# Attention's output leaves PSUM by one plain copy per chunk; rms_g is applied with the reciprocal root on VectorE

## The chip, the cores and the metric

The kernel runs on one core of a Trainium2 chip. The metric is the device time of one execution in microseconds (us), as the median of several runs. The engines are TensorE (PE in the profile; PEld is its weight load), VectorE (DVE), ScalarE (ACT), GpSimd (POOL) and SyncE (SP), each with a queue of its own that it works through in order.

## The reference

Linear attention with a decay per head, followed by a gated layer with RMS normalisation and a second layer:

```python
# _attn_ref, per step t; B, H, S, D = 2, 8, 768, 64
state = gamma * state + k_t v_t^T
y[t] = q_t state / sqrt(D)
# x: y as (B * S, H * D) = (1536, 512)
rms = np.sqrt(np.mean(x * x, axis=-1, keepdims=True) + 1e-06)
xn = x / rms * rms_g
g = xn @ w_gate
silu = g * (1.0 / (1.0 + np.exp(-g)))
x = (silu * (xn @ w_val)) @ w_out          # w_gate, w_val: 512 x 1536
h = x @ w_in                               # w_in: 512 x 2048
out = np.maximum(0.01 * h, h) @ w_out2
```

All of it is in float32; `rms_g` has one value for each of the 512 features.

## The kernel before

The 1536 tokens are cut into 12 chunks of 128. Each chunk's attention output `y` is one PSUM bank of 128 partitions by 4 x 128: features lie on the partitions in four groups of 128 (two heads each), tokens along the free dimension. Three blocks of four chunks make the buffers `xg` (float32, 128 x 4 x 512), and each block is then split into two parts for the matrix products, a rounded high part `xh` and the rest `xl`.

Up to some 67 us the attention of late chunks, the normalisation of earlier ones, the conversion of the first weights and the first products of the layer run side by side. The order of all of this is written out by hand in a table of short tokens (`ORDER`, from L49), which is issued under a manual schedule: each engine gets its instructions in the order of the tokens. What follows the table (from about 92 us on some engines) is planned in the program and ordered automatically. The normalisation of a pair of chunks passes these steps, with the token's name in brackets:

- squares (`sq`, L325) on ScalarE: the square of `y`, one instruction per chunk.
- gains (`xg`, L333) on ScalarE: `y` times `rms_g` into `xg`, one instruction for each of the four feature groups, since the gain is a per-partition scalar that differs between groups.
- first_sum and second_sum (`fa`, `sa`, L340 and L345) on VectorE: the squares of the four feature groups added together.
- total (`to`, L354) on TensorE: the sum over the partitions; mean (`me`, L361) on VectorE; rsqrt (`rs`, L365) on GpSimd, a power of -0.5.
- spread (`sp`, L371) on TensorE: the reciprocal root copied to all partitions, into the PSUM bank `norm`.
- scaled (`xs`, L388) on VectorE: `xg` times `norm` in place, for both chunks and all four groups in one instruction of 128 x 1024.
- high (`hi`, L395) on ScalarE and rest (`lo`, L402) on VectorE: the split into `xh` and `xl`.

The tokens of a pair carry the pair's number, so that `xs4` is scaled of chunks 8 and 9. The matrix products of the layer's first half are the matmuls of L657: eight on `xh`, then four on `xl`. L1062 multiplies the activated gate product by the value product, L258 is the decay mask on the attention scores, and L534 to L560 convert weights. The pairs stand in the table as `xs0` to `xs5`; the table's lines 54 to 58 hold five of them:

```
he7 v0:H xs0 kd10 he6 me1 sa5 g1:3 sc10 v0:L sq6 g1:4 sq7 ou9 fa6 xg6 sc11 rs1 up9 ds10 xg7 yi8 ds11 g1:H yi9 hi0 qs11
ou10 o0:P he8 lo0 to2 up10 sq8 he9 fa7 xg8 sa7 sa6 me2 g1:L to3 sq9 sp1 fa8 rs2 me3 xg9 yi10 xs1 rs3 v1:P yi11 fa9
o0:1 sa9 hi1 sp2 v1:1 sa8 he10 v1:2 xs2 he11 sq10 v1:3 xg10 layers Mg00 lo1 hi2 v1:4 Ng00 sq11 lo2 o1:P Mg10 fa11 xg11
fa10 o1:1 sa10 sa11 v1:H Ng10 o0:2 o1:2 Cg00 v1:L sp3 Cg10 o1:3 to4 xs3 Mv00 me4 o0:3 hi3 o1:4 Nv00 lo3 o1:H Mv10 o1:L
Cv00 rs4 o0:4 Uo00 sp4 Lo00 o0:H to5 Nv10 g2:P xs4 Mg01 me5 o0:L hi4 rs5 Cv10 lo4 Uo10 sp5 g3:P Ng01 Lo10 Mg11 xs5
```

`Mg00` is the high half and `Ng00` the low half of the first product of the layer.

Of the kernel before, what the change touches and what calls it, by code (L numbers as in the profile page):

```python
# [13 lines left out]
AF = mybir.ActivationFunctionType  # L14
ALU = mybir.AluOpType
AX = mybir.AxisListType

P = 128
CH = 128
# [47 lines left out]
def chain_kernel(ctx: ExitStack, tc: tile.TileContext, qk_t, kv, w1, w2, mask, qdec, kdec, sdec, rms_g, ident, out):  # L67
    nc = tc.nc
    NCHUNK = kv.shape[0]
    NPAIR = 4  # L70
# [31 lines left out]
    g_sb = const.tile([P, NPAIR, 1], F32, name="g_sb")  # L102
# [10 lines left out]
    def acc_bank(i, name):  # L113
        return ps_acc.tile([P, 512], F32, tag=f"acc{i}", name=name)
# [4 lines left out]
    def by_pair(t):  # L119
        return t.rearrange("p (a t) -> p a t", a=NPAIR)  # L120


    ch = {}
    xh, xl, xg = {}, {}, {}
# [17 lines left out]
    nrm = {"bank": acc_bank(3, "norm")}  # L142
# [65 lines left out]
    def block_of(c):  # L208
        return max(i for i in range(NB) if offs[i] <= c * CH)
# [117 lines left out]
    def gains(c):  # L327
        b = block_of(c)
        if b not in xg:
            xg[b] = xp.tile([P, NPAIR, BLOCKS[b]], F32, tag=f"acc{b}", name=f"xg{b}")  # L330
        o = c * CH - offs[b]
        for a in range(NPAIR):
            nc.scalar.activation(  # L333
                out=xg[b][:, a, o:o + CH], in_=ch[c]["y"][:, a * CH:(a + 1) * CH], func=AF.Copy, scale=g_sb[:, a, :]
            )

    def first_sum(c):
        s = ch[c]
# [40 lines left out]
    def span(cs):  # L379
        b = block_of(cs[0])  # L380
        o = cs[0] * CH - offs[b]
        return b, slice(o, o + len(cs) * CH)

    def scaled(cs):
        b, o = span(cs)
        x = xg[b][:, :, o]
        r = nrm[cs]["bank"][:, None, :len(cs) * CH].to_broadcast([P, NPAIR, len(cs) * CH])
        nc.vector.tensor_tensor(out=x, in0=x, in1=r, op=ALU.mult)  # L388

    def high(cs):  # L390
        b, o = span(cs)
# [923 lines left out]
    def layers():  # L1315
# [3 lines left out]
    by_chunk = {  # L1319
        "sc": scores, "ds": decay_scores, "yi": before, "ou": outer, "up": update, "kd": decay_k, "qs": decay_q,  # L1320
        "he": heads, "wm": lambda c: keep_warm(c, 4), "sq": squares, "xg": gains, "fa": first_sum, "sa": second_sum,
    }
    by_pair_of = {"to": total, "me": mean, "rs": rsqrt, "sp": spread, "xs": scaled, "hi": high, "lo": rest}
    alone = {
        "open": reopen, "layers": layers, "load": lambda: load("q11", "k11"),
# [136 lines left out]
```

## Time and profile before

| | us |
|---|---|
| median of 3 runs | 576.85 (576.67 to 576.88) |
| profiled execution, its own time | 577.89 |
| span of that execution | 576.1 |
| busy: TensorE | 567.6 (99%) |
| busy: VectorE | 501.7 (87%) |
| busy: ScalarE | 408.2 (71%) |
| busy: GpSimd | 42.8 (7%) |

A busy share is an average over the whole span. What a change is worth is read from the stretch in which it lies: who waits there, and for whom. In a list of instructions the second number is the duration; the distance to the next start can be shorter, since an instruction may start before the one ahead of it has ended.

### The profile page before, as it was taken

How to read it: one execution, taken by the hardware profiler on the slowest of the kernel's cores; microseconds unless marked ns; L12 is line 12 of the kernel's file. 1: busy time of each engine (PE TensorE's matmuls, PEld its weight loads, DVE VectorE, ACT ScalarE, POOL GpSimd, SP SyncE). 2: the span in 40 equal slices, each digit the busy share in tenths (PEclk: the TensorE clock that was granted, in tenths of full speed). 3: DMA queues.
4: the chain of work that ended last, by engine and by line, in shares of the span. 5: the costliest groups of instructions: out<-in, count | busy, mean ns of one | idle time of the engine just before them, and what ended most of it. 6: DMA issues, size and time to landing. Idle time of an engine off the chain costs nothing.

```text
span 576.1 us, 8549 instructions
## 1 busy us (share of the span) xinstructions
PE 567.6 (99%) x3091; PEld 466.5 (81%) x3091; DVE 501.7 (87%) x983; ACT 408.2 (71%) x747; POOL 42.8 (7%) x49
## 2 busy tenths in 40 slices
PE   8999999999999999999999999999999999999997
PEld 6888788888888888888788878788888788888886
DVE  8899989985776899985899999999999979995692
ACT  4799768987656556976647699989858885676330
POOL 3341300010000000010000200000100020002100
PEclk9999999999999999999999999999999999999999
DMA  8991422442211122226220322123512343101555
GB/s 341 406 353 38 147 73 75 146 147 73 74 53 32 63 74 66 81 84 136 73 75 0 91 56 96 54 89 129 180 41 74 113 85 96 39 0 27 120 88 133
DMA packets 35114, 59.28 MB, mean 103 GB/s; under 512 B 19264, under 2 KB 19520, under 8 KB 35072
## 3 DMA queue, kind: packets, MB, share of 16 engines
q1 hardware_dynamic: 31584, 51.39, 26.8%
q0 software_dynamic: 3200, 7.34, 6.2%
q8 instruction: 24, 0.39, 0.3%
q14 instruction: 18, 0.15, 0.1%
q10 hardware_dynamic: 288, 0.01, 0.0%
HBM read 50.34 MB, written 8.39 MB: 102 GB/s over the span
## 4 chain that ended last, share of the span: by engine, by line
PE 79%; DVE 8%; DMA 7%; ACT 4%; issue 1%; POOL 0%; DVEq 0%; ACTq 0%; POOLq 0%
PE X L913 11%; PE Z L913 8%; PE i L657 7%; PE ao L692 7%; PE iX L1116 7%; PE ap L692 6%; PE v L657 6%; PE g L657 6%; PE vX L1116 4%; PE gX L1116 4%; PE iZ L1116 3%; PE vZ L1116 2%; PE ao L775 2%; PE gZ L1116 2%; DMA raw_v<-in_w 2%; DMA qkv<-in_kv 2%
## 5 line engine op out<-in xcount | busy, mean ns | idle before, releaser
L692 PE MATMUL ap<-w_p,gp_0h 128*128 128x512 f32 (+1 forms) x128 | 38.8, 383 | 0.0
L657 PE MATMUL i<-x2h,w_i 128*128 128x512 f32 x128 | 31.9, 389 | 0.0
L657 PE MATMUL g<-xh,w_g 128*128 128x512 f32 x128 | 31.8, 390 | 0.0
L657 PE MATMUL v<-xh,w_v 128*128 128x512 f32 x128 | 31.7, 390 | 0.0
L657 PEld LDWEIGHTS g<-xh,w_g 128*128 128x128 f32 x128 | 23.9, 188 | 5.2 <-issue 0.2
L657 PEld LDWEIGHTS i<-x2h,w_i 128*128 128x128 f32 x128 | 24.0, 188 | 5.0
L657 PEld LDWEIGHTS v<-xh,w_v 128*128 128x128 f32 x128 | 23.9, 188 | 5.0
L692 PEld LDWEIGHTS ap<-w_p,gp_0h 128*128 128x128 f32 x128 | 23.8, 188 | 4.8
L692 PE MATMUL ap<-w_p,gp_0l 128*128 128x512 f32 x64 | 24.5, 382 | 0.0
L1052 ACT ACTIVATE more<-i 128x512 f32<-128x512 f32 x16 | 9.5, 596 | 20.0 <-PE i L657 20.0
L692 PE MATMUL ao<-go_0h,w_o 128*128 128x512 f32 x64 | 21.0, 389 | 0.0
L1116 PE MATMUL iX<-th,w_si 128*128 128x512 f32 x64 | 20.6, 399 | 0.2 <-ACT is L1133 0.2
L1116 PE MATMUL iZ<-x2h,w_si 128*128 128x512 f32 x64 | 20.5, 392 | 0.0
L560 DVE TENSOR_TENSOR w_o<-wa_o,w_o 128x512 fp32r<-128x512 f32 x12 | 8.2, 687 | 13.8 <-ACT w_o L556 13.8
L657 PE MATMUL g<-xl,w_g 128*128 128x512 f32 x64 | 17.2, 391 | 0.0
L657 PE MATMUL v<-xl,w_v 128*128 128x512 f32 x64 | 17.2, 391 | 0.0
L944 DVE TENSOR_TENSOR y2acc<-X,y2acc 128x512 f32<-128x512 f32 x26 | 17.1, 684 | 0.0
L657 PE MATMUL i<-x2l,w_i 128*128 128x512 f32 x64 | 17.1, 389 | 0.0
L258 DVE TENSOR_TENSOR a<-sc,mask_sb 128x1024 f32<-128x1024 f32 (+1 forms) x13 | 14.5, 1137 | 1.1 <-PE sc L246 1.0
L983 POOL DMA_DIRECT2D out<-more x8 | 7.1, 1030 | 113.6 <-ACT more L979 113.4
L1116 PEld LDWEIGHTS iX<-th,w_si 128*128 128x128 f32 x64 | 11.7, 188 | 4.2 <-ACT is L1133 1.2
L609 ACT ACTIVATE wb_i<-raw_i 128x512 int32<-128x512 uint32 x16 | 10.7, 671 | 5.8 <-DMA raw_i<-in_w 2.4
(385 smaller groups left out, 1860.2 us busy)
## 6 DMA issues: line engine op xcount, KB each, us to landing
raw_i<-in_w SPq DMA_DIRECT2D x16, 512.0 KB, 3.5
raw_g<-in_w SPq DMA_DIRECT2D x12, 512.0 KB, 3.6
raw_v<-in_w SPq DMA_DIRECT2D x12, 512.0 KB, 3.5
raw_o<-in_w SPq DMA_DIRECT2D x12, 512.0 KB, 3.5
raw_p<-in_w SPq DMA_DIRECT2D x11, 512.0 KB, 3.5
qkT<-in_qk_t SPq DMA_DIRECT2D x7, 512.0 KB, 8.4
kv<-in_kv SPq DMA_DIRECT2D x7, 512.0 KB, 9.2
out<-more POOLq DMA_DIRECT2D x12, 256.0 KB, 4.6
```

The source lines that it names most:

```text
L258: nc.vector.tensor_tensor(out=s["a"][:, j], in0=s["sc"][:, j], in1=mask_sb[:, j], op=ALU.mult)
L560: v.tensor_tensor(out=u[:, 1, :], in0=a, in1=u[:, 0, :].bitcast(F32), op=ALU.subtract)
L609: nc.scalar.activation(out=m, in_=low.bitcast(U32), func=AF.Copy, scale=2.0 ** -29)
L657: nc.tensor.matmul(out=dst, lhsT=lhs, rhs=rhs, start=(n == 0), stop=(n == len(pairs) - 1), skip_group_check=True)
L692: nc.tensor.matmul(out=dst, lhsT=lhs, rhs=rhs[:, c:c + cut], start=(start and n == 0), stop=(stop and n == 2), skip_group_check=True,)
L775: nc.tensor.matmul(out=acc["b"][m], lhsT=lhs, rhs=rhs, start=(e == fs[0] and n == 0), stop=(e == fs[-1] and n == 2), skip_group_check=True,)
L913: nc.tensor.matmul(out=acc[side][m], lhsT=lhs, rhs=rhs, start=(start and f == fs[0] and k == 0), stop=(f == fs[-2] and k == 2), skip_group ...
L944: nc.vector.tensor_tensor(out=dst, in0=banks[m], in1=dst, op=ALU.add)
L983: nc.gpsimd.dma_start(out=rows, in_=dst, accum_op=ALU.add)
L1052: nc.scalar.activation(out=a, in_=x, func=AF.Prelu, alpha=0.01)
L1116: nc.tensor.matmul(out=dst, lhsT=lhs, rhs=rhs, start=(start and n == 0), stop=(n == 5), skip_group_check=True)
```

## The change

The four gain copies of a chunk become one copy without a gain, over all four feature groups. Scaled is cut into four instructions, one per feature group, each of which multiplies `xg` by the gain (a per-partition scalar) and by `norm`. Nothing else is written differently.

```diff
-        for a in range(NPAIR):
-            nc.scalar.activation(
-                out=xg[b][:, a, o:o + CH], in_=ch[c]["y"][:, a * CH:(a + 1) * CH], func=AF.Copy, scale=g_sb[:, a, :]
-            )
+        nc.scalar.activation(out=xg[b][:, :, o:o + CH], in_=by_pair(ch[c]["y"]), func=AF.Copy)
...
-        x = xg[b][:, :, o]
-        r = nrm[cs]["bank"][:, None, :len(cs) * CH].to_broadcast([P, NPAIR, len(cs) * CH])
-        nc.vector.tensor_tensor(out=x, in0=x, in1=r, op=ALU.mult)
+        r = nrm[cs]["bank"][:, :len(cs) * CH]
+        for a in range(NPAIR):
+            x = xg[b][:, a, o]
+            nc.vector.scalar_tensor_tensor(out=x, in0=x, scalar=g_sb[:, a, :], in1=r, op0=ALU.mult, op1=ALU.mult)
```

On ScalarE, around the high part of chunks 0 and 1 (`xh0`), the queue before holds these rows; the number after a name is that of a chunk or a weight, and the last number is that of a buffer:

```order
L325 ACTIVATE sq6_759<-y6_732 128x512 [waits PE_49]
L325 ACTIVATE sq7_762<-y7_671 128x512
L333 ACTIVATE xg1_629<-y6_732,g_sb_102 128x128 x4
L333 ACTIVATE xg1_629<-y7_671,g_sb_102 128x128 x4
L556 ACTIVATE w_g1_474<-wa_g1_475 128x512 [waits DVE_49]
L395 ACTIVATE xh0_815<-xg0_314 128x4x256
```

The same place now:

```order
L325 ACTIVATE sq6_744<-y6_717 128x512 [waits PE_49]
L325 ACTIVATE sq7_747<-y7_653 128x512
L332 ACTIVATE xg1_617<-y6_717 128x4x128
L332 ACTIVATE xg1_617<-y7_653 128x4x128
L554 ACTIVATE w_g1_468<-wa_g1_469 128x512 [waits DVE_49]
L393 ACTIVATE xh0_794<-xg0_314 128x4x256
```

Eight instructions ahead of the high part have become two, and the order is the same.

On VectorE, at scaled of chunks 8 and 9, the queue before holds:

```order
L1062 TENSOR_TENSOR g0_0_1011<-v0_0_1028,g0_0_1011 128x512 [waits PE_49]
L553 ISA wa_o0_829<-wa_o0_829,wb_o0_830 128x1024
L729 TENSOR_TENSOR go_0_0l_1070<-g0_0_1011,go_0_0h_1064 128x512 [waits Activation_49,Pool_49]
L388 TENSOR_TENSOR xg2_859<-xg2_859,norm_112 128x4x256 [waits DMAHW1_49,PE_49]
L361 TENSOR_SCALAR na10_1099<-norm_112 128x2 [waits Pool_49]
```

and now:

```order
L1060 TENSOR_TENSOR g0_0_984<-v0_0_1004,g0_0_984 128x512 [waits PE_49]
L551 ISA wa_o0_808<-wa_o0_808,wb_o0_809 128x1024
L727 TENSOR_TENSOR go_0_0l_1046<-g0_0_984,go_0_0h_1040 128x512 [waits Activation_49,Pool_49]
L386 SCALAR_TENSOR_TENSOR xg2_838<-xg2_838,g_sb_102,norm_112 128x256 [waits DMAHW1_49,PE_49]
L386 SCALAR_TENSOR_TENSOR xg2_838<-xg2_838,g_sb_102,norm_112 128x256 x3
L358 TENSOR_SCALAR na10_1078<-norm_112 128x2 [waits Pool_49]
```

One instruction has become four, of which the first alone waits, and the mean of chunks 10 and 11 (`na10`) stands behind them as before. The other five pairs change in the same way. In the part that is ordered automatically, some 50 instructions on VectorE and ScalarE change places with near neighbours.

## Rows read from the trace of the kernel before

**Rows 1.** The page, its head and the engines' busy times.

```profile
span 576.1 us, 8549 instructions
...
PE 567.6 (99%) x3091; PEld 466.5 (81%) x3091; DVE 501.7 (87%) x983; ACT 408.2 (71%) x747; POOL 42.8 (7%) x49
```

**Rows 2.** Stretches: length, busy us and instructions of each engine, clock, DMA share, GB/s.

```profile
51.00:67.00 16.00, 15.77 (x101) 12.21 (x97) 15.55 (x28) 12.29 (x24) 4.41 (x2) 1.00 0.35 103
67.00:100.00 33.00, 33.00 (x147) 27.31 (x146) 30.96 (x52) 24.42 (x39) 0.00 (x0) 1.00 0.31 94
```

**Rows 3.** Waits of TensorE after 80 us: total, times, longest, in us.

```profile
PE vX L1116 <- ACT more L1133: 0.9, 1, 0.9
```

**Rows 4.** The chain of waits up to 80 us: start, length, what.

```profile
65.05 0.16 DVE na L361
...
65.35 1.01 POOL nr L365
...
66.40 0.66 PE norm L371 x8
```

**Rows 5.** ScalarE's instructions in order: start, duration, line, tiles, count.

```profile
38.63 1.05 ACT L325 ACTIVATE sq<-y 128x512 f32<-128x512 f32 x2
39.59 2.15 ACT L333 ACTIVATE xg<-y,g_sb 128x128 f32<-128x128 f32 x8
41.59 0.67 ACT L556 ACTIVATE w_g<-wa_g 128x512 fp32r<-128x512 f32 x1
42.11 1.10 ACT L395 ACTIVATE xh<-xg 128x1024 fp32r<-128x1024 f32 x1
```

**Rows 6.** VectorE's instructions in order; in brackets idle time before, and its releaser.

```profile
36.35 1.21 DVE L388 TENSOR_TENSOR xg<-xg,norm 128x1024 f32<-128x1024 f32 x1
37.48 0.15 DVE L361 TENSOR_SCALAR na<-norm 128x2 f32<-128x2 f32 x1
...
40.24 2.34 DVE L258 TENSOR_TENSOR a<-sc,mask_sb 128x1024 f32<-128x1024 f32 x2
43.24 1.38 DVE L402 TENSOR_TENSOR xl<-xg,xh 128x1024 fp32r<-128x1024 f32 x1 [0.66 <-ACT xh L395]
...
51.56 1.22 DVE L402 TENSOR_TENSOR xl<-xg,xh 128x1024 fp32r<-128x1024 f32 x1
...
61.85 0.69 DVE L1062 TENSOR_TENSOR g<-v,g 128x512 f32<-128x512 f32 x1
...
70.90 1.22 DVE L402 TENSOR_TENSOR xl<-xg,xh 128x1024 fp32r<-128x1024 f32 x1
...
92.75 1.29 DVE L1062 TENSOR_TENSOR g<-v,g 128x512 f32<-128x512 f32 x2 [0.47 <-PE v L657]
```

**Rows 7.** VectorE's instructions in order, small ones early in the program.

```profile
4.63 0.17 DVE L182 TENSOR_TENSOR kdecs<-kdecs,turn 128x8 f32<-128x8 f32 x1
4.83 0.35 DVE L184 SCALAR_TENSOR_TENSOR mask_sb<-rows,kdecs,state 128x128 f32<-128x128 f32 x1
5.09 0.16 DVE L182 TENSOR_TENSOR kdecs<-kdecs,turn 128x8 f32<-128x8 f32 x1
5.17 0.35 DVE L184 SCALAR_TENSOR_TENSOR mask_sb<-rows,kdecs,state 128x128 f32<-128x128 f32 x1
...
29.81 0.76 DVE L340 TENSOR_TENSOR sq<-sq 128x256 f32<-128x256 f32 x2
30.48 0.29 DVE L345 TENSOR_TENSOR ss<-sq 128x128 f32<-128x128 f32 x1
```

**Rows 8.** TensorE's matmuls in order.

```profile
53.07 1.07 PE L657 MATMUL g<-xl,w_g 128*128 128x512 f32 x4
...
62.54 0.66 PE L371 MATMUL norm<-ident_sb,nr 128*64 128x128 f32 x8 [0.16 <-POOL nr L365]
...
75.32 1.07 PE L657 MATMUL g<-xl,w_g 128*128 128x512 f32 x4
```

**Rows 9.** GpSimd's instructions in order.

```profile
59.08 3.41 POOL L365 TENSOR_TENSOR nr<-na,expo 128x2 f32<-128x2 f32 x1 [11.28 <-DVE na L361]
```

## The prediction

> **What bounds the kernel now.** The page comes first: the profiled span is 576.1 us and TensorE is busy for 567.6 of it [rows 1]. Eight and a half microseconds are all that TensorE leaves, so I ask where they lie. The stage table answers: from 67 to 100 us TensorE is busy for 33.00 of 33.00, in 51 to 67 us for 15.77 of 16, with VectorE at 15.55 of 16 beside it and ScalarE at 12.29 [rows 2]. A change that moves the point near 67 us at which TensorE begins to run without a gap moves the end with it, unless a later wait takes the difference up. The longest TensorE wait after 80 us is one of 0.9 us, on a ScalarE instruction [rows 3], which reads a product of TensorE's own and so shifts with it.
>
> The chain of waits then says who sets that point. Its part before TensorE's long run ends in this order: the mean of chunks 10 and 11 on VectorE (L361, 65.05, queued behind scaled of chunks 8 and 9), the power on GpSimd (65.35 to 66.36), and TensorE's spread (L371, 66.40), from where it stays on TensorE [rows 4]. So around 60 us VectorE leads and TensorE follows at a distance of hundredths. Both operations that the change makes dearer or cheaper lie before this point.
>
> **The change, part by part.** *ScalarE loses time.* Eight gain copies (two chunks) run from 39.59 to the next start at 41.59, 2.00 us, so 1.00 us a chunk; two squares, which read the same 128x512 from PSUM in one instruction each, take from 38.63 to 39.59, 0.48 us each [rows 5]. I price the new copy as such a square: each of the 12 chunks gives ScalarE about 0.5 us back, 6 us in all. What is this worth? Only where somebody waits for ScalarE behind it. There is one such place: VectorE starts rest of chunks 0 and 1 (L402) at 43.24, after high (L395) that ScalarE starts at 42.11 [rows 5, 6]. The two mask products before it start at 40.24, and one 128x1024 product holds VectorE for 37.48 - 36.35 = 1.13 us, so VectorE was free at 42.50 and stood for 0.74 us [rows 6]. In the new order two gain copies stand ahead of this high; with 1.0 us less it starts near 41.1 and ends near 42.2, so this wait goes whole. Elsewhere ScalarE's gain costs and gives nothing: the later copies have slack before spread and heads.
>
> *VectorE gains work.* Six products of 128x1024 (L388, 1.21 us of duration) become 24 of 128x256 with a per-partition scalar [rows 6]. The trace has no such size, so I bound it. Two plain additions of 128x256 start at 29.81 and the next instruction at 30.48, 0.335 us each. The one scalar-tensor-tensor with a per-partition scalar is L184, on 128x128: its duration is 0.35 us, that of a plain addition of this size at 30.48 is 0.29 [rows 7]. The scalar therefore costs about 0.06, and I take 0.335 + 0.06 = 0.395 for each, 1.58 for four, 0.45 more per pair of chunks than the 1.13 of now. Lower bound: the scalar is fetched behind the instruction before it, 4 x 0.335 = 1.34, +0.21 per pair. Upper bound: the starts no longer overlap the ends (L184 lasts 0.35 and the next starts 5.09 - 4.83 = 0.26 after it, an overlap of 0.09), 4 x 0.485 = 1.94, +0.81 per pair. I stay with +0.45 because L184 is the same instruction form on the same engine. That one operand of it is in PSUM, as norm is in the new one, I cost at nothing: 1.13 for 1024 elements with PSUM and 0.335 for 256 without it lie on one line, of 0.265 per 256 elements and 0.07 per instruction.
>
> *Along the path.* VectorE's queue, counted as lateness against now: scaled of chunks 0 and 1 adds 0.45; the wait of 0.74 at 43.24 swallows it, and VectorE is then 0.29 early. TensorE, whose sums and spread hang on VectorE there, is early with it. Scaled of 2 and 3 makes it 0.16 late, of 4 and 5, which stands before rest of 2 and 3 (51.56), 0.61 late. That rest ends at 52.78 now and TensorE's low products start at 53.07 [rows 6, 8]; it will end near 53.4, so the first layer starts its low half some 0.35 to 0.55 late, a first stall. Scaled of 6 and 7: 1.06 late. After it come the mean of 8 and 9 and the power for it: GpSimd holds that power for 3.41 us, to 62.49, 0.64 after VectorE's L1062 has started at 61.85 [rows 6, 9]. Whatever holds it, both of its neighbours on VectorE come 1.06 later, in an unchanged order, so TensorE's spread at 62.54 [rows 8], which waits already, goes to 63.6. Behind it on TensorE stand the sums of 10 and 11 and all of the layer. Scaled of 8 and 9 adds the fifth 0.45: the mean of 10 and 11, the power and the spread at 66.40 come 1.51 late. The sixth, of 10 and 11, is after the last spread; its high and low parts feed a product at 75.32, while the low part was ready at 72.12 [rows 6, 8]: 3.2 us of cover, and 0.45 more would be lost only if that were gone. VectorE's own lateness of 0.45 beyond TensorE's is given back at 92.75, where it waits 0.47 for TensorE [rows 6].
>
> The sum is 5 x 0.45 - 0.74 = +1.5 us. Against the profiled execution's own 577.89 us (576.1 of span and 1.8 around it) this is 579.4; the median of the runs is 1.04 lower than that execution, and I carry the difference over to it: 576.85 + 1.5 = **578.35 us**, +0.26%. The bounds give 5 x 0.21 - 0.74 = +0.3 and 5 x 0.81 - 0.74 = +3.3.
>
> *A rule of the skill against the row.* In the rows the instruction behind L184 starts 0.09 us before L184 has ended, and so do the 128x256 products (0.76 us for two at a spacing of 0.67) [rows 7]. The Trainium skill (VectorE: DVE Perf Modes, The DRAIN you can't avoid) says that the next instruction doesn't start until the pipe has emptied, and under Rules for kernel authors that the count of instructions is what to keep small. By that, 24 instead of 6 would each show their whole duration, and the sum would be that of the upper bound, +3.3; by the rows it is +1.5.
>
> The automatic part behind the written order (from 92 us on) is reordered in places over some 50 instructions on VectorE and ScalarE, as conversions of weights change places with each other. TensorE has no idle stretch there and its order is the same, and its products use weights made microseconds earlier; I cost it at nothing, with a few tenths either way if that cover is thinner than it looks.
>
> **The rivals.** *Each scalar is fetched for free.* Four instructions then cost +0.21 per pair and the end moves by +0.3: 577.1 us, no measurable change. For it: L184 follows tiny instructions in the trace, so a fetch behind a long one is not shown. Against it: L184's own duration has the 0.06 in it (0.35 against 0.29 for the plain product of that size) [rows 7]. A change counts as none within 0.2%, 1.15 us, which is about what a measurement of this kernel can tell; the point from which the forecast leaves that band is 0.38 per pair.
>
> *ScalarE's relief wins.* The place is rest of chunks 0 and 1 at 43.24, the price 0.74, and it decides if four new instructions cost less than 0.15 over the one old. They would have to cost 0.32 each, less than a plain 128x256 product; at no extra at all the time is 576.1 us. More than 0.74 isn't to be had there, so even this is inside the band. Faster by over 0.2% needs a second wait on ScalarE that I don't see.
>
> *The instructions don't overlap.* All four write the same tile; if each waits for the end of the last, +3.3 us, 580.15 us. For it: L184 at 4.83 starts 0.20 after the 4.63 of an instruction whose result it needs, whereas at 5.17, with no such need, it starts 0.08 after the 5.09 [rows 7]. Against it: the four write different quarters, and the new order shows a wait only on the first.
>
> **How the numbers follow.** Forecast 0.50 (578 to 579.2), free fetch 0.27, no overlap 0.13, ScalarE's relief 0.10. The range leaves out the end of the no-overlap case and of the relief case: 576.9 to 579.8 us. Slower by over 0.2% is the forecast (nearly all), the no-overlap case: 0.61; within 0.2% the free fetch and most of the relief: 0.34; faster 0.05.
>
> **What would show it.** In the changed profile: 12 copies near 0.6 us with 0.5 us of spacing; 24 scalar-tensor-tensor instructions near 0.48 us, spaced by 0.395 (0.335 and 0.485 are the rivals'); no VectorE wait before rest of chunks 0 and 1; idle stretches on TensorE of about 0.6 before the first low product, 0.7 more before the spread of 8 and 9, and 0.45 before that of 10 and 11; that spread at 67.9; TensorE without a gap from there. I am wrong if TensorE's spread of 10 and 11 comes before 67.5, if VectorE is faster on these than on plain products, or if a TensorE wait after 70 us grows or goes.

## The result, and the profile after

The changed kernel takes **579.98 us** (median of six runs), the kernel before 576.76 us (six runs). One of the six executions took 1468.89 us, far outside the others, and counts in that median; the other five (578.96 to 580.76) have a median of 579.26, and the ratio is theirs: 1.0051, interval [1.004, 1.0062]. The kernel is slower, as forecast, but by 2.5 us (by 3.2 with the outlying execution in the median) where 1.5 was expected. A second measurement on another occasion, below, gave 579.05 us and 1.0033 [1.0021, 1.0045], 2.1 us more than before. The profiled execution took 579.24 us, 577.5 of them span. The page's head and busy times, beside [rows 1]:

```profile
span 577.5 us, 8536 instructions
...
PE 567.5 (98%) x3091; PEld 466.6 (81%) x3091; DVE 504.7 (87%) x1001; ACT 401.9 (70%) x711; POOL 44.9 (8%) x49
```

TensorE does the same work in 1.4 us more of span. VectorE has 18 instructions and 3.0 us more, ScalarE 36 instructions and 6.3 us less. ScalarE's queue in order, at the place of [rows 5]:

```profile
38.75 1.06 ACT L325 ACTIVATE sq<-y 128x512 f32<-128x512 f32 x2
39.70 1.06 ACT L332 ACTIVATE xg<-y 128x512 f32<-128x512 f32 x2
40.66 0.63 ACT L554 ACTIVATE w_g<-wa_g 128x512 fp32r<-128x512 f32 x1
41.18 1.06 ACT L393 ACTIVATE xh<-xg 128x1024 fp32r<-128x1024 f32 x1
```

Two copies take 40.66 - 39.70 = 0.96 us of the queue, 0.48 each, and the high part of chunks 0 and 1 starts at 41.18 instead of 42.11. VectorE's queue in order, beside [rows 6]:

```profile
36.47 1.64 DVE L386 SCALAR_TENSOR_TENSOR xg<-xg,g_sb,norm 128x256 f32<-128x256 f32 x4
38.03 0.15 DVE L358 TENSOR_SCALAR na<-norm 128x2 f32<-128x2 f32 x1
...
43.03 1.45 DVE L400 TENSOR_TENSOR xl<-xg,xh 128x1024 fp32r<-128x1024 f32 x1
...
58.45 1.65 DVE L386 SCALAR_TENSOR_TENSOR xg<-xg,g_sb,norm 128x256 f32<-128x256 f32 x4
60.02 0.15 DVE L358 TENSOR_SCALAR na<-norm 128x2 f32<-128x2 f32 x1
...
65.08 1.65 DVE L386 SCALAR_TENSOR_TENSOR xg<-xg,g_sb,norm 128x256 f32<-128x256 f32 x4
66.65 0.15 DVE L358 TENSOR_SCALAR na<-norm 128x2 f32<-128x2 f32 x1
```

Four instructions hold the queue for 38.03 - 36.47 = 1.56 us, 0.39 each; before it was 1.13. The wait of rest of chunks 0 and 1 for ScalarE is gone: at 43.03 stands no bracket, where [rows 6] has 0.66. What TensorE makes of it, its matmuls in order, beside [rows 8]:

```profile
53.56 1.20 PE L655 MATMUL g<-xl,w_g 128*128 128x512 f32 x4 [0.51 <-DVE xl L400]
...
63.71 0.66 PE L368 MATMUL norm<-ident_sb,nr 128*64 128x128 f32 x8 [0.70 <-POOL nr L362]
...
68.00 0.66 PE L368 MATMUL norm<-ident_sb,nr 128*64 128x128 f32 x8 [0.51 <-POOL nr L362]
```

These are the three stalls that were forecast: 0.51, 0.70 and 0.51 us. Between the two profiled executions TensorE runs 0.49 us later at the first (53.56 against 53.07), 1.17 at the second (63.71 against 62.54) and 1.60 at the third (68.00 against 66.40). After that the stretches, as in [rows 2], show TensorE without a gap:

```profile
51.00:68.00 17.00, 15.28 (x89) 11.64 (x88) 16.83 (x35) 10.93 (x17) 4.41 (x2) 1.00 0.30 95
68.00:100.00 32.00, 32.00 (x146) 26.43 (x147) 29.73 (x51) 23.02 (x36) 0.00 (x0) 1.00 0.31 98
```

The difference stays at 1.56 us up to 277 us. There the profiled execution of before has its wait of 0.9 us [rows 3], which is absent in that of after, and from there TensorE is only 0.46 us behind (its last matmul starts at 572.53 against 572.07). But the span is 1.4 us longer. The rest of the time lies behind TensorE's last product. The waits of SyncE's queue in the last stretch of the changed kernel (total, times, longest) have this row:

```profile
SPq L1456 <- DMA out<-partial: 1.9, 3, 1.2
```

The landing of its last transfers, from issue, by the view of the tile `partial`:

```profile
DMA to landing us min/median/max: 2.0/2.1/2.7
```

SyncE's wait in the kernel before:

```profile
SPq L1458 <- DMA out<-partial: 1.0, 3, 0.4
```

And the landing there:

```profile
DMA to landing us min/median/max: 1.9/2.0/2.1
```

The last of the five transfers takes the 2.7 us; in the kernel before the last takes 1.9 and the longest 2.1. The end of the program waits 1.2 us for it instead of 0.4. TensorE's last matmul, in the kernel before:

```profile
572.07 0.28 PE L692 MATMUL tail<-w_p,gp_0l 128*128 128x256 f32 x1
```

and in the changed one:

```profile
572.53 0.28 PE L690 MATMUL tail<-w_p,gp_0l 128*128 128x256 f32 x1
```

From its start to the end of the span it is 577.5 - 572.53 = 4.97 us, against 576.1 - 572.07 = 4.03. I call this stretch the tail. No term of the prediction covers it.

### The profile page after: what moved, and what is told of

The parts are those of the page before. It is cut to its first block, busy times and chain, and to the rows that moved or that the text cites. A ratio compares the mean times of both kernels' runs of the same rounds, so it can differ in the third digit from the quotient of the medians.

```text
span 577.5 us, 8536 instructions
## 1 busy us (share of the span) xinstructions
PE 567.5 (98%) x3091; PEld 466.6 (81%) x3091; DVE 504.7 (87%) x1001; ACT 401.9 (70%) x711; POOL 44.9 (8%) x49
## 4 chain that ended last, share of the span: by engine, by line
PE 83%; DVE 8%; DMA 5%; ACT 3%; issue 1%; POOL 0%; SPq 0%; DVEq 0%; POOLq 0%; ACTq 0%
PE X L911 11%; PE Z L911 8%; PE ao L690 8%; PE i L655 7%; PE v L655 7%; PE iX L1114 7%; PE ap L690 6%; PE g L655 6%; PE vX L1114 5%; PE gX L1114 5%; PE iZ L1114 3%; PE vZ L1114 2%; PE gZ L1114 2%; DMA qkv<-in_qk_t 2%; PE ao L773 2%; DMA qkv<-in_kv 2%
## 5 line engine op out<-in xcount | busy, mean ns | idle before, releaser
L655 PEld LDWEIGHTS g<-xl,w_g 128*128 128x128 f32 x64 | 11.9, 188 | 3.5 <-DVE xl L400 0.9
```

Source lines behind the costliest of these rows:

```text
L655: nc.tensor.matmul(out=dst, lhsT=lhs, rhs=rhs, start=(n == 0), stop=(n == len(pairs) - 1), skip_group_check=True)
```

## The experiments

Two theories about the part up to 70 us: the forecast's (0.39 to 0.40 for each new instruction, less the wait that goes), and its rivals. Two about the tail: A, it grows because a packet of the queue that fetches instructions falls beside the last transfers; B, it belongs to the changed computation itself. The packet of theory A is this row of the changed kernel's DMA queues between 574.5 and 575.5 us, where the kernel before has none so late:

```profile
q14 instruction: 1, 0.01, 2.9%
```

The ratio of each run is against the kernel before on the same chip.

**The two kernels again (b_again, a_again).** No edit.

> The kernel before, unchanged. Theory: its profiled execution (577.89 us) is 1.1 us above its timed runs because of one wait of TensorE near 277 us, behind weight transfers of 8 us; another profiled execution may lack it, then its span is near 575.0 us and its own time near 576.8. Rival: the wait belongs to every execution, and the profiled one is longer for another reason; then the wait is there again and the span is 576.1. In both the ratio to itself is 1.000 within 0.0003.

> The changed kernel, unchanged. Theory: 1.56 us of the loss are TensorE's later start near 68 us, the rest lies behind TensorE's last product, where the last transfer lands 0.7 us later with an instruction fetch beside it; then the timed runs are 579.0 to 579.3 (+2.5), and an execution near 580.7 shows the wait near 277 us on top. Rival: the rest is a wait in the middle that comes and goes; then this profile shows TensorE losing more than 1.6 us before its last product and a last transfer as short as before.

Before: 577.13 us beside 576.98, ratio 0.9998 [0.9989, 1.0006]. After: 579.05, ratio 1.0033 [1.0021, 1.0045]. The wait near 277 us comes and goes. In the first profile of before, TensorE's product `vX` starts 1.24 us after the matmul ahead of it:

```profile
276.41 0.39 PE L1116 MATMUL vY<-xl,w_v 128*128 128x512 f32 x1
277.65 0.74 PE L1116 MATMUL vX<-th,w_sv 128*128 128x512 f32 x2 [0.85 <-ACT more L1133]
```

In b_again it starts 0.49 after it:

```profile
276.37 0.39 PE L1116 MATMUL vY<-xl,w_v 128*128 128x512 f32 x1
276.86 0.73 PE L1116 MATMUL vX<-th,w_sv 128*128 128x512 f32 x2
```

In nine of the fourteen profiles the distance is 0.22 to 0.24, and nothing is lost; so the wait is 1.01 us in the first profile of before, 0.26 in b_again and 0.11 in a_again (0.34). The 1.01 accounts for that execution's own time of 577.89 us, 1.04 above the median. The ScalarE instruction that it waits for stands behind a conversion of weights, which waited for their transfer by 2.38 us in before, 1.62 in b_again and 1.48 in a_again; it starts 9.1 us behind that conversion in all three.

TensorE's spread of chunks 10 and 11 and its last matmul, in b_again:

```profile
66.38 0.66 PE L371 MATMUL norm<-ident_sb,nr 128*64 128x128 f32 x8 [0.28 <-POOL nr L365]
...
571.34 0.28 PE L692 MATMUL tail<-w_p,gp_0l 128*128 128x256 f32 x1
```

and in a_again:

```profile
67.74 0.66 PE L368 MATMUL norm<-ident_sb,nr 128*64 128x128 f32 x8 [0.51 <-POOL nr L362]
...
572.41 0.28 PE L690 MATMUL tail<-w_p,gp_0l 128*128 128x256 f32 x1
```

TensorE is 1.36 us later at the spread and 1.07 at the last matmul; 0.15 of the 0.29 between them is the wait near 277 us. The tails are 4.89 and 4.06. 1.07 + 0.83 = 1.9, the difference of the spans (577.3 and 575.4).

**The plain copy alone (copy_only).** Scaled stays one instruction:

```diff
-        for a in range(NPAIR):
-            nc.scalar.activation(out=xg[b][:, a, o:o + CH], in_=..., func=AF.Copy, scale=g_sb[:, a, :])
+        nc.scalar.activation(out=xg[b][:, :, o:o + CH], in_=by_pair(ch[c]["y"]), func=AF.Copy)
```

> ScalarE's half alone: one plain copy per chunk, scaled as before, so that rms_g is left out of the result. Theory: VectorE's wait of 0.74 us at 43.24 goes, nothing else does, so TensorE's spread of chunks 10 and 11 comes at 65.7 to 66.1 instead of 66.40 and the time is 0.3 to 0.74 us lower, 576.0 to 576.5 (plus up to 0.9 if the last transfer is late here too). Rival: ScalarE's 6 us reach the end by more, 575.5 or less. Other rival: nothing waits for ScalarE, 576.8.

576.75 us, ratio 0.9993 [0.9984, 1.0002]: no difference, where 0.3 to 0.74 us less was expected. VectorE's queue shows the wait gone:

```profile
36.70 1.20 DVE L385 TENSOR_TENSOR xg<-xg,norm 128x1024 f32<-128x1024 f32 x1
...
40.59 2.34 DVE L258 TENSOR_TENSOR a<-sc,mask_sb 128x1024 f32<-128x1024 f32 x2
42.85 1.63 DVE L399 TENSOR_TENSOR xl<-xg,xh 128x1024 fp32r<-128x1024 f32 x1
```

From scaled to rest it is 42.85 - 36.70 = 6.15 us, in b_again 43.22 - 36.34 = 6.88: 0.73 less, the term of 0.74. Half of it was already lost at the start, which lay 0.36 later in this execution, and TensorE's spread of chunks 10 and 11 came only 0.12 earlier (66.26).

**The new instructions alone (stt_only).** The four gain copies stay as they were, ahead of the four scalar-tensor-tensor instructions.

```diff
+        for a in range(NPAIR):
+            nc.scalar.activation(out=xg[b][:, a, o:o + CH], in_=..., func=AF.Copy, scale=g_sb[:, a, :])
-        nc.scalar.activation(out=xg[b][:, :, o:o + CH], in_=by_pair(ch[c]["y"]), func=AF.Copy)
```

(against the changed kernel)

> VectorE's half alone: four instructions with the scalar, and the gain copies of before, so that rms_g is applied twice. Theory: the first pair's 0.43 us go into VectorE's wait for ScalarE at 43.24, four pairs reach TensorE, spread of 10 and 11 at 66.39 + 1.72 = 68.1, 0.4 us later than with the plain copy; time 579.4 with 0.85 of tail. Rival: the plain copies are worth nothing, five pairs count in both: the same time as the changed kernel, 579.05.

579.87 us, ratio 1.0049 [1.0037, 1.0061]. TensorE's spread of chunks 10 and 11 stands at 68.25, 0.51 later than in a_again and 1.87 later than in b_again; rest of chunks 0 and 1 waits again, for 0.24 us at 43.34. The tail is 4.86. So all of the loss comes from VectorE's side, and the plain copy gives back about half a microsecond of it on TensorE.

**Four plain products instead of one (split_plain).** The gain copies stay; scaled becomes four products of 128x256 without the scalar:

```diff
-        x = xg[b][:, :, o]
-        r = nrm[cs]["bank"][:, None, :len(cs) * CH].to_broadcast([P, NPAIR, len(cs) * CH])
-        nc.vector.tensor_tensor(out=x, in0=x, in1=r, op=ALU.mult)
+        r = nrm[cs]["bank"][:, :len(cs) * CH]
+        for a in range(NPAIR):
+            x = xg[b][:, a, o]
+            nc.vector.tensor_tensor(out=x, in0=x, in1=r, op=ALU.mult)
```

> Scaled cut into four plain products of 128x256 without the scalar, gains as before, the result unchanged. Theory: 0.335 us of spacing each, +0.21 per pair; the first is taken up by VectorE's wait for ScalarE, four reach TensorE, spread of 10 and 11 at +0.84, time 577.6 (plus up to 0.9 behind the last product). Rival: the count of instructions is what costs, the scalar nothing: spacing 0.39 as in the changed kernel, +1.7 us, 578.5.

578.54 us, ratio 1.0024 [1.0015, 1.0033]. VectorE's queue:

```profile
36.35 1.40 DVE L389 TENSOR_TENSOR xg<-xg,norm 128x256 f32<-128x256 f32 x4
37.67 0.14 DVE L361 TENSOR_SCALAR na<-norm 128x2 f32<-128x2 f32 x1
...
43.24 1.38 DVE L403 TENSOR_TENSOR xl<-xg,xh 128x1024 fp32r<-128x1024 f32 x1 [0.47 <-ACT xh L396]
```

Four plain products hold the queue for 1.32 us, 0.33 each. Of the 0.43 us that a pair costs more (1.56 - 1.13), the cut into four is 0.19 and the scalar operand 0.24, 0.06 per instruction. On TensorE the spread of chunks 10 and 11 is 0.79 later than in b_again (67.17), and the tail is 4.80: a kernel with neither the scalar nor the plain copy, but with as many VectorE instructions (1001), has the long tail too.

**Instructions of nothing, early (before_pad_v, after_pad_v).** Memsets of 128x1 on VectorE, 18 in the kernel before and twice 20 in the changed one, put into the written order:

```diff
+    def pad():
+        for _ in range(18):
+            nc.vector.memset(ready[:, :1], 0.0)
...
-... qs5 sc5 ds4 g0:P ...
+... qs5 sc5 pad ds4 g0:P ...
```

> The kernel before with 18 memsets of one element per partition added on VectorE, ahead of the decay mask of chunk 4, where VectorE waits 0.67 us; they write an unused tile. Theory: the 0.85 us behind TensorE's last product come from the place at which VectorE's stream of instructions reaches its last fetched piece, which 18 more instructions move into the last transfer; then TensorE's rows stay as before (spread of 10 and 11 near 66.4), one instruction packet lies in the last microseconds and the time is 577.8. Rival: the late last transfer belongs to the changed order of the work; then 577.0 and no such packet.

> The changed kernel with 40 such memsets, 20 at each of two waits of VectorE (ahead of the decay mask of chunk 4 and of the key decay of chunk 6). Theory: they move the fetch of the last piece ahead of the last transfer, so that the tail behind TensorE's last product is 4.05 us again instead of 4.9 and the time falls to 578.2, although instructions are added. Rival: the tail stays at 4.9 and the time at 579.1 or a little above.

579.95 us, 1.0054 [1.0038, 1.0071], and 582.96 us, 1.0104 [1.0091, 1.0117]; both far over what either theory gave. The memsets were not free: VectorE's queue in the second kernel shows 0.12 us each (2.33 over 19),

```profile
17.74 2.33 DVE L202 MEMSET ready<- 128x1 f32 x19
...
27.04 2.31 DVE L202 MEMSET ready<- 128x1 f32 x19
```

and around 18 and 27 us VectorE's work is on the way to the first spreads. TensorE is 3.0 us later than in b_again at its last matmul, and 4.1 later than in a_again. As times they tell nothing of the tail; their tails do. With 18 memsets the packet lies in the last 0.1 us and the tail is 4.25, the last transfers landing after 1.9 to 2.1 us as before; with 40 no packet lies in the tail and it is 4.03, although this is the changed kernel.

**Instructions of nothing, late (before_late, after_late).** The same idea at a place that I took for harmless, 24 memsets in the kernel before and 40 in the changed one:

```diff
     def times(key, x, a):
         nc.vector.tensor_tensor(out=a, in0=x, in1=a, op=ALU.mult)
+        late.append(key)
+        if 8 <= len(late) < 28:
+            for _ in range(2):
+                nc.vector.memset(ready[:, :1], 0.0)
```

(of after_late; before_late has 20 for 28)

> The changed kernel with 40 memsets of 128x1 more on VectorE, two behind each of 20 gate products between about 120 and 290 us, where TensorE never waited for VectorE. What it tells apart: why the stretch behind TensorE's last product is 4.9 us in the changed kernel and 4.0 in the kernel before. Theory A (a packet of instructions that happens to be fetched beside the last transfers): 40 more instructions move the packet's place, as the 40 at the start did; the stretch falls to 4.0 to 4.1, no packet of the instruction queue lies within 4 us of the end, the landing of the last transfers has no 2.7 us, and the time is 578.2 (578.0 to 578.5) beside 579.05 for the changed kernel. Theory B (the stretch is longer because of the new instructions themselves, the fewer ScalarE instructions or the lateness): it stays at 4.8 to 5.0 and the time at 579.0 to 579.2. Rival C: the memsets cost on the path: over 579.3, with TensorE later from 120 us on.

> The kernel before with 24 memsets of 128x1 more on VectorE, two behind each of 12 gate products between about 120 and 290 us. Theory A (a packet of instructions beside the last transfers): the kernel before gets the packet in its last 4 us that it lacked; if it lies ahead of the last transfers' landing the stretch behind TensorE's last product is 4.8 to 4.9 and the time 577.6 (577.4 to 577.9), if it lies in the last 0.5 us 4.1 to 4.3 and 576.9. Theory B (only the changed computation lengthens that stretch): 4.0 to 4.1 and the time of the kernel before, 576.8.

581.49 us, 1.0081 [1.0068, 1.0094], and 580.57 us, 1.0063 [1.0045, 1.008]. Both times are over what theories A and B gave. Rival C, a cost on the path, comes nearest, but TensorE is not late from 120 us on: the memsets didn't run where they were written. They wait for nothing, and the ordering of the program moved them to its start, between 3.8 and 12.7 us in before_late and 3.8 and 21.1 in after_late, from the building of the masks on, where VectorE's queue is full. The first of them in after_late:

```profile
3.20 0.69 DVE L165 TENSOR_TENSOR rows<-rows,steps_of 128x512 f32<-128x512 f32 x1
3.84 1.08 DVE L1066 MEMSET ready<- 128x1 f32 x9
4.97 0.22 DVE L178 TENSOR_SCALAR state<-ident_sb 128x128 f32<-128x128 f32 x1
```

TensorE's last matmul is 3.2 us later than in a_again and 2.9 later than in b_again. (Two of the six runs of before_late stand at 579.1 us, 1.6 below the profiled one; what they lack isn't shown.) The tails are theory A's in both. The changed kernel with 40 memsets has a tail of 4.01, and among its waits SyncE's is back at that of before:

```profile
SPq L1462 <- DMA out<-partial: 1.0, 3, 0.3
```

The kernel before with 24 has a tail of 4.77, and its last transfers, from the DMA queues in the stretch from 574.5 to 575.5 us, share it with a packet of instructions:

```profile
q14 instruction: 1, 0.01, 1.9%
...
out<-partial SPq DMA_DIRECT2D x1, 256.0 KB, 2.9
out<-partial SPq DMA_DIRECT2D x1, 128.0 KB, 2.7
```

The five last transfers are issued between 573.18 and 575.74 us here, and the packet falls between 575.0 and 575.3, while all of them but the last are under way or being issued; they take 2.3 to 2.9 us, all five longer than the 1.9 to 2.1 of the kernel before. In the changed kernel only the last of the five, issued at 573.80 and under way when the packet comes, takes 2.7; the four ahead of it take 2.0 to 2.1.

Every profile has a packet of this queue 6.5 to 8.3 us before the end; what differs is whether one more comes behind it. The tails of all profiled executions (one for each run; the packet's place from stretches of half a microsecond, counted back from the end):

| kernel | VectorE instructions | last packet before the end, us | tail, us |
|---|---|---|---|
| before; b_again; copy_only | 983 | 6.4 to 7.6 | 4.03; 4.06; 4.04 |
| mixed; mixed_means | 986 | 6.3 to 7.0 | 4.00; 4.10 |
| after_pad_v; after_late | 1041 | 6.1 to 7.0 | 4.03; 4.01 |
| before_pad_v | 1001 | 0.1 | 4.25 |
| before_late | 1007 | 3.5 to 4.0 | 4.77 |
| split_plain; after_means; stt_only | 1001 | 2.0 to 2.7 | 4.80; 4.85; 4.86 |
| a_again; after | 1001 | 2.0 to 2.8 | 4.89; 4.97 |

**The means first (after_means).** In the changed kernel the means of chunks 8, 9 and 10, 11 are issued ahead of the scaled product that they stood behind:

```diff
-... o1:3 to4 xs3 Mv00 me4 o0:3 ...
+... o1:3 to4 me4 xs3 Mv00 o0:3 ...
-... g2:P xs4 Mg01 me5 o0:L ...
+... g2:P me5 xs4 Mg01 o0:L ...
```

> The changed kernel with the mean of chunks 8 and 9 ahead of scaled of 6 and 7, and that of 10 and 11 ahead of scaled of 8 and 9. Theory: TensorE's two stalls at spread (0.70 and 0.51 us) hang on the mean queued behind the four new instructions on VectorE; with the mean ahead they go, the stall of 0.51 before the first low product stays, spread of 10 and 11 comes near 66.9 to 67.1 instead of 67.74 to 68.00 and the time is 578.0 (with 0.85 of tail). Rival: spread waits for the four instructions themselves, which read the bank that it writes; then it comes no earlier than 67.5 and the time is 578.8 to 579.1.

578.11 us, 1.0019 [1.001, 1.0028]: 1.25 us over the kernel before, where a_again was 2.07 over it. TensorE's spread of chunks 10 and 11 stands at 66.85 instead of 67.74, and what it waits for is no longer GpSimd but VectorE's scaled product:

```profile
62.84 0.66 PE L368 MATMUL norm<-ident_sb,nr 128*64 128x128 f32 x8
...
66.85 0.66 PE L368 MATMUL norm<-ident_sb,nr 128*64 128x128 f32 x8 [0.23 <-DVE xg L386]
```

So the lateness of the last two scaled products reached TensorE by way of the mean and GpSimd's power, as the prediction had it. What remains over before, 1.25 us, is the tail (4.85, 0.79 more than in b_again) and a spread that is still 0.47 later than in b_again (66.85 against 66.38). The last matmuls start together all the same (571.35 and 571.34): 0.26 of the 0.47 is the wait near 277 us, which b_again has and after_means lacks.

**The new form for one pair (mixed, mixed_means).** Plain copy and four instructions for chunks 6 and 7 only; mixed_means also has the means first. (The expectation calls it the first pair; it is the fourth of the six, and its gain copies are the ones ahead of the high part of chunks 0 and 1.)

```diff
+        if c in (6, 7):
+            nc.scalar.activation(out=xg[b][:, :, o:o + CH], in_=by_pair(ch[c]["y"]), func=AF.Copy)
+            return
...
+        if cs == (6, 7):
+            r = nrm[cs]["bank"][:, :len(cs) * CH]
+            for a in range(NPAIR):
+                x = xg[b][:, a, o]
+                nc.vector.scalar_tensor_tensor(out=x, in0=x, scalar=g_sb[:, a, :], in1=r, op0=ALU.mult, op1=ALU.mult)
+            return
```

> The new form only for the first pair of chunks (6 and 7): plain copy and four scalar-tensor-tensor instructions there, the old form for the other five pairs. By the terms of the prediction: the pair costs VectorE 0.43 to 0.45 us more, ahead of a wait for ScalarE of 0.65 to 0.74 us that is gone; the other five pairs cost nothing more, so that TensorE's product g<-xl of 53.1 us starts 0.2 to 0.3 earlier, and the spread of chunks 10 and 11 lies within 0.3 of that before. Time 576.5 (576.2 to 576.9); with three instructions more on VectorE no packet moves into the last transfers. Rival (the early products are not on the path, or the start's own jitter covers it): 576.8, the same as before. Rival (cost of the packet): 577.5.

> As the kernel with the new form only for chunks 6 and 7, and the means of the pairs that follow issued ahead of the scaled products of the pairs ahead of them at two places, so that GpSimd's root starts about 1.2 us earlier. In the changed kernel that order took 0.87 us off the spread of chunks 10 and 11. Here, where GpSimd's root is waited for 0.2 to 0.3 us in all, it can give no more than that: 576.3 (576.0 to 576.7), against 576.5 without it. Rival (the product of chunks 8 and 9, later by the mean's own 0.1 us, delays more than the wait): 576.8 or over.

mixed: 576.98 us, 1.0009 [0.9995, 1.0023], the same as before, where 0.3 less was expected. The low products start 0.25 us earlier than in b_again (52.81), but the pair's own 0.44 falls between there and the power for chunks 8 and 9, which starts 0.18 later (59.24 against 59.06). That spread waits 0.57 and lies 0.39 later (62.70), since the power also took 3.41 us where b_again has 1.07; in the first profile of before, with 3.41, it stands at 62.54. mixed_means: **576.17 us, 0.9987 [0.9978, 0.9995]**, faster than both kernels. The spreads of TensorE wait no more; its matmuls in mixed_means:

```profile
61.99 0.66 PE L374 MATMUL norm<-ident_sb,nr 128*64 128x128 f32 x8
...
65.70 0.66 PE L374 MATMUL norm<-ident_sb,nr 128*64 128x128 f32 x8
```

The last spread lies 0.68 earlier than in b_again (66.38) and 0.86 earlier than in mixed (66.56), where 0.3 was expected: GpSimd's powers not only start earlier, they take 0.69 us each, in mixed 3.41 and 1.00. Whether the means first would do as much in the kernel before, without the new form, wasn't tried.

## Why the prediction was right, and what it lacked

**What sets the end.** Right. From the spread of chunks 10 and 11 on TensorE runs without a gap, but for 0.2 us in every profile and the wait near 277 us in some, and what is late there is late to the last product, less a few tenths (1.36 us at the spread, 1.07 at the last matmul, between the two kernels run again).

**ScalarE's relief.** Right in size and place: 0.48 per copy as priced, the wait of 0.74 gone, 0.73 by copy_only.

**The price of the new instruction.** 0.395 forecast, 0.39 measured; 0.45 per pair forecast, 0.43 measured. The scalar costs the 0.06 read off L184. The rivals' spacings, 0.335 and 0.485, are both excluded: the median duration is 0.472 and the starts lie 0.39 apart, so each start overlaps an end by 0.08. The Trainium skill (VectorE: DVE Perf Modes, The DRAIN you can't avoid), which the prediction weighed against its rows, says there too that a next instruction that is not held starts earlier; these four rows agree with that exception and not with the rule by itself.

**The lateness along the path.** The prediction's steps and what the profiled pair and the runs again show:

| step | forecast | after - before | a_again - b_again |
|---|---|---|---|
| first low product | +0.35 to 0.55 | +0.49 | +0.24 |
| spread of 8 and 9 | +1.06 | +1.17 | +1.14 |
| spread of 10 and 11 | +1.51 | +1.60 | +1.36 |

Of the 1.14 at the spread of 8 and 9, 0.22 is the power's 3.41 us in a_again, where b_again has 1.07: the power itself starts 0.92 later (59.98 against 59.06). The spread of 10 and 11 was to come at 67.9 and came at 68.00 and 67.74. No overlap would have made the sum +3.3 and a free fetch +0.3.

**The step that failed: the sum had no term behind TensorE's last product.** I took what is late at 67 us as the change of the end. The runs show a second term, +0.8 to 0.9 us in the tail, in every kernel in which a packet of the instruction queue comes 2 to 4 us before the end. It is not the scalar (split_plain), not the plain copy (stt_only has the long tail without it) and not the lateness (after_pad_v is 4.1 us later than a_again and has the short tail): the memsets take it away from the changed kernel and give it to the kernel before. Theory A holds; B falls. That the packet slows the last transfers, rather than coming with something else that does, is read from its place in fourteen profiles and from which transfers are under way when it comes; why one packet costs 0.8 us isn't shown.

**A second wrong step, of small cost here.** I wrote of the 0.9 us wait on ScalarE that it shifts with TensorE's own product [rows 3]. It doesn't: it hangs on a transfer of weights as well, and comes and goes from execution to execution of the same kernel (1.01 and 0.26 us in the two profiles of before; 0.51 in stt_only, 0.26 in mixed, 0.11 in a_again, none in the other nine). The prediction named a TensorE wait after 70 us that grows or goes as a sign that it was wrong, and this one went.

With both terms, 1.07 to 1.6 and 0.8 to 0.9, the change is worth 1.9 to 2.5 us, and the second measurement (2.1) lies in this. The same sum, lateness at the spread plus longer tail, gives 0.79 + 0.74 = 1.53 us for split_plain, which measured 1.56 over before, and 0.47 + 0.79 = 1.26 for after_means, which measured 1.25. The first measurement's 579.98 lies 0.2 us over the range that was given; its five ordinary runs (579.26) and the second measurement (579.05) lie inside. That they do is luck in part: the room above the forecast of 578.35 was there for dearer instructions and a thinner cover, and 0.8 us of what was measured is the tail, of which the prediction knew nothing. Two of the first measurement's five runs stand at 580.7 us; what they had that the profiled 579.24 lacked stays open.

## What to carry to other kernels

Moving work off an engine is worth what someone waits for it (0.73 us here of the 6 that ScalarE saved), and costs the engine that takes it in full where that engine leads: four instructions for one cost 0.19 us for the cut and 0.24 for four scalar operands, five times over. Before such a change, look for what stands behind the dearer instruction in its queue and can go first: the mean of 0.15 us ahead of the product took 0.8 to 0.9 us off the changed kernel. And look behind the last product too: a number of instructions can decide what is fetched beside the last transfers, and instructions that wait for nothing run where the ordering puts them, which need not be where they were written.

## What was unexpected of the hardware

- One packet of the instruction queue among the last transfers goes with a tail of 4.8 to 5.0 us instead of 4.0 to 4.1; where the last packet comes 6 to 8 us before the end the tail is 4.0 to 4.1, and with one in the last 0.1 us it was 4.25.
- GpSimd's power of 128x2 took 3.41 us or about 1.0, and 0.69 once the mean stood first. GpSimd's instructions in the changed kernel:

```profile
60.25 3.41 POOL L362 TENSOR_TENSOR nr<-na,expo 128x2 f32<-128x2 f32 x1 [12.58 <-DVE na L358]
66.95 1.00 POOL L362 TENSOR_TENSOR nr<-na,expo 128x2 f32<-128x2 f32 x1 [3.29 <-DVE na L358]
```

  VectorE's two products that read PSUM:

```profile
63.03 0.68 DVE L1060 TENSOR_TENSOR g<-v,g 128x512 f32<-128x512 f32 x1
...
67.32 0.68 DVE L1060 TENSOR_TENSOR g<-v,g 128x512 f32<-128x512 f32 x1
```

  The first power, the one of [rows 9], ends at 63.66, 0.63 us after VectorE turned at 63.03 to a product that reads PSUM; from 60.09 until then VectorE's instructions are conversions and a rest, whose inputs lie in SBUF. The second ends at 67.95, again 0.63 after such a product (67.32). With the mean first the power runs beside the scaled product, which reads `norm` from PSUM, in 0.69; the first of the two in after_means:

```profile
58.56 0.69 POOL L362 TENSOR_TENSOR nr<-na,expo 128x2 f32<-128x2 f32 x1 [11.02 <-DVE na L358]
```

  The Trainium skill (Advanced Engine Details and Errata, GPSIMD Details) says that GpSimd shares an interface with VectorE and conflicts with instructions of it that have two SBUF inputs; these rows agree. In b_again the power of chunks 8 and 9, started at 59.06 and so 0.02 us earlier than in [rows 9], took 1.07, as it did in before_pad_v and before_late: what lets it through there isn't shown.
- In a row of them, a memset of 128x1 held VectorE for 0.12 us, a third of a plain product of 128x256 (0.33).
